# Three vector passes of a weight conversion moved behind a gate's first step, with one POOL sum in place of two halves

## The chip, the cores and the metric

The kernel runs on one core of a Trainium2 chip. The time is the device time of one execution in microseconds (us). The kernel before takes 814.9 us, the median of three executions (814.84 to 814.9).

The core's engines run side by side, each through its own list of instructions in order: TensorE (PE in the profile, its weight loads PEld), VectorE (DVE), ScalarE (ACT), GpSimd (POOL) and SyncE (SP). Semaphores order them against each other. DMAs are issued from the lists of SP, ACT and POOL.

## The reference, cut to what matters

```python
# x (8, 8, 512, 64), state (8, 8, 32, 64); per batch and head:
scores = scale * x @ state.T;  a = softmax(scores);   xread = a @ state
scores2 = scale * state @ x.T; a2 = softmax(scores2); sread = a2 @ x
x = concatenate([xread, sread], axis=2)      # -> (8 * 544, 512) tokens
h = x @ w_in                                 # w_in (512, 2048)
g = h * cos(h)
out = g @ w_out                              # w_out (2048, 512)
```

x and state arrive as float32. w_in and w_out arrive as float64, and the chip computes in float32, so each weight has to be turned from 64 bits into 32 on the way in.

## The kernel before, in words

**Order of the work.** The lists of all engines are written out by hand. A prologue prepares batch 0. Then a loop of 16 steps per batch follows, one step for each slice of 128 of the 2048 hidden features, and 16 more steps for the state tokens. Step s does, in this order of code: PE multiplies the hidden tile (`hidden`, L443) of 128 features by 512 tokens; the gate follows in four parts, ACT's pass that rounds (`gate`, L449), DVE's distance (`gate2`, L452), ACT's magnitude and sine (`gate3`, L457 and L458) and DVE's product (`gate4`, L464). PE's output product of a tile (`output`, L508) comes three or four steps later. Hidden tiles have two PSUM banks, so the hidden product of step s+2 writes the bank that the product (L464) of step s has read.

**Attention** of the next batch is spread over the steps by `plan`: its parts go on the lists at five places of a step, `go(0)` to `go(4)`, where `go(1)` and `go(2)` are ACT's parts and `go(3)` and `go(4)` DVE's. `products` (L295) multiplies a block of w_in by the states, and its copies (L422 on DVE, L424 on ACT) make the weights of the hidden product. `max1`, `max2` (with a small scaling, L327), `spread1`, `shift`, `exps`, `sums` (with L351 and L352), `norm1` and `keep` are the softmax.

**Weight loads.** Eighteen loads (two more at the end) bring w_in and w_out as raw 64-bit words into one of three buffers, on SP (`fetch`, L190). `convert_part` makes 32-bit words of each: ACT takes the high words ("1", L218) and the low words ("2", L221, into `low`), DVE limits ("a", L225), shifts ("b", L227) and puts in the sign ("c", L230), POOL adds the low words ("d", L240). A buffer is fetched anew after "c". Loads 0 to 3 have 512 elements per partition, all later ones 1024. The table `conv_at` gives load 4 + i to a step; steps 0 to 8 and 10 to 14 have one. In its step a load gets "1", "2" and, at the end of the step, "a" and "b"; "c" and "d" come in the next step, between distance and product. From load 4 on POOL's "d" is two instructions of 512.

**Prologue.** All eight heads of batch 0 are loaded on SP; the states of batches 0 to 3 half on ACT, half on POOL; then SP fetches raw loads 0 to 4 and the other states. Raw loads 0 and 1 share a buffer, 2 and 3 another. PE turns three quarters of the tokens, then the states, then the last quarter; scores follow, then matmuls on zeros (`warm`), while DVE and ACT go through softmax and the first conversions.

**Later.** From step 15 on POOL makes sums of blocks of w_out (`blocks`, L775) and differences of gated tiles (L470).

Of the kernel before, what the change touches and what calls it, by code (L numbers as in the profile page):

```python
# [10 lines left out]
I32 = mybir.dt.int32  # L11
U32 = mybir.dt.uint32
ALU = mybir.AluOpType
# [10 lines left out]
def kernel(  # L24
# [8 lines left out]
    nc = tc.nc  # L33
# [5 lines left out]
    NK = Dm // P  # L39
# [43 lines left out]
    x_b = consts.tile([P, NC, H, D], F32)  # L83
# [10 lines left out]
    low = s4.rearrange("p f d -> p (f d)")  # L94
    low = [low[:, 2 * WC * i:2 * WC * i + 2 * WC] for i in range(2)]
    RG = 4 * WC * 2 // S // 2
    raw_at = [g_all[:, NG - RG * (3 - i):NG - RG * (2 - i)] for i in range(3)]
    raw_at = [r.rearrange("p t s -> p (t s)") for r in raw_at]
# [2 lines left out]

    stT = consts.tile([P, B, P], F32)

    def load_x(b):

        src = x[b].rearrange("h (c p) d -> p c h d", p=P)
        for h in range(H):
            nc.sync.dma_start(out=x_b[:, :, h], in_=src[:, :, h])


    zeros = g_all[:, 0]
# [1 line left out]

    load_x(0)
    st_src = state.rearrange("b (k j) n d -> j k n b d", j=2)

    def load_state(half, queues):
        b = slice(4 * half, 4 * half + 4)  # L120
        for k in range(NK):
            for j in range(2):
                queues[j].dma_start(
                    out=st[Ns * k:Ns * k + Ns, b, D * j:D * j + D],
                    in_=st_src[j, k, :, b])
# [7 lines left out]
    acc = [[ops.tile([P, S], F32, name=f"o{m}{ch}") for ch in range(2)]  # L133
           for m in range(2)]

    def states(half, to):
        for i in range(4):
            nc.tensor.transpose(out=to[:, P * i:P * i + P],
                                in_=st[:, 4 * half + i, :], identity=ident)

    def states_kept(half, to):
        dst = slice(4 * half, 4 * half + 4)
        src = to.rearrange("p (b m) -> p b m", b=4)
        nc.vector.tensor_scalar(stT[:, dst], src, 1.0 / TWO_PI, None,
                                op0=ALU.mult)
# [22 lines left out]
    N_LOADS = len(loads)  # L168
# [5 lines left out]
    n_fetched = 0  # L174

    def fetch(n):
        nonlocal n_fetched
        while n_fetched < n:
            dst, src = loads[n_fetched]
            if f64:  # L180
                m, w = dst.shape[1:]

                at_, c0 = (n_fetched - 2) % 3, 0
                if n_fetched < 4:
                    at_, c0 = n_fetched // 2, n_fetched % 2 * 2 * m * w
                if n_fetched >= N_LOADS:
                    at_ = 3 + n_fetched - N_LOADS
                raw = raw_at[at_].bitcast(I32)[:, c0:c0 + 2 * m * w]
                raw = raw.rearrange("p (m f) -> p m f", m=m)
                nc.sync.dma_start(out=raw, in_=src.bitcast(I32))  # L190
                raws[n_fetched] = raw.rearrange("p m (f w) -> p m f w", w=2)
            else:
                nc.sync.dma_start(out=dst, in_=src)
            n_fetched += 1
# [6 lines left out]
    def convert(i, parts):  # L201

        if i < len(loads) and f64:
            for p in parts:
                convert_part(i, p)
        if "c" in parts and i not in (1, 2) and i + 3 < N_LOADS:
            fetch(max(i + 4, 6))

    def convert_part(i, p):
        raw, dst = raws[i], loads[i][0]
        bits = dst.bitcast(I32)
        m, w = dst.shape[1:]
        c0 = m * w if i in (2, 3) else 0
        e = low[i % 2][:, c0:c0 + m * w].rearrange("p (m f) -> p m f", m=m)
        if p == "1":
            nc.scalar.activation(dst, raw.bitcast(F32)[:, :, :, 1],  # L218
                                 func=ACTF.Abs)
        elif p == "2":  # L220
            nc.scalar.activation(e, raw.bitcast(U32)[:, :, :, 0],  # L221
                                 func=ACTF.Copy, scale=2.0 ** -51, bias=2.0)
        elif p == "a":
            engine = nc.gpsimd if i == 1 else nc.vector
            engine.tensor_scalar(dst, dst, 2.0 ** -15, None, op0=ALU.max)  # L225
        elif p == "b":
            nc.vector.tensor_scalar(bits, bits, 3, None,  # L227
                                    op0=ALU.logical_shift_left)
        elif p == "c":
            nc.vector.scalar_tensor_tensor(out=bits, in0=raw[:, :, :, 1],  # L230
                                           scalar=-2 ** 31, in1=bits,
                                           op0=ALU.bitwise_and,
                                           op1=ALU.bitwise_xor)
        else:


            n = 1 if i < 4 else 2
            for j in range(n):
                r = slice(m * j // n, m * j // n + m // n)
                nc.gpsimd.tensor_tensor(bits[:, r], bits[:, r],  # L240
                                        e.bitcast(I32)[:, r], op=ALU.add)

# [3 lines left out]
    class Attention:  # L248
# [27 lines left out]
        def tokens_kept(self, k):  # L276
            nc.scalar.copy(self.xT[:, k], at[k % 2])

        def all_tokens(self, k0, k1):

            xp = [acc[k // 2][k % 2] for k in range(NK)]
            for k in range(k0, k1):
                for c in range(NC):
                    self.turn_x(k, c, xp[k])
                if k % 2 == 0:
                    nc.scalar.copy(self.xT[:, k], xp[k])
                else:
                    nc.vector.tensor_copy(self.xT[:, k], xp[k])
# [139 lines left out]
    def part(b, name, *args):  # L428

        if b not in attn:  # L430
            attn[b] = Attention(b)
        getattr(attn[b], name)(*args)
        if (name, args) == ("reads", (1,)) and b + 1 < B:
            load_x(b + 1)


    class Tile:
# [2 lines left out]
    def hidden(t):  # L440
        t.hp = hps.tile([P, S], F32, name="h")[:, 0:t.n]
        for i in range(t.kn):
            nc.tensor.matmul(out=t.hp, lhsT=t.lhs(i), rhs=t.rhs(i),  # L443
                             start=(i == 0), stop=(i == t.kn - 1))

    def gate(t):

        t.q = msb.tile([P, S], F32, name="q")[:, 0:t.n]
        nc.scalar.activation(t.q, t.hp, func=ACTF.Copy, bias=MAGIC)  # L449
# [11 lines left out]
    def gate4(t):  # L461
        t.slot = g_free.pop(0)
        t.g = g_all[:, t.slot, 0:t.n]
        nc.vector.tensor_tensor(t.g, t.hp, t.q, op=ALU.mult)  # L464
# [7 lines left out]
    MAIN, SIDE = 0, 1  # L472
# [195 lines left out]
    def warm(n, to):  # L668

        for _ in range(n):  # L670
            nc.tensor.matmul(out=to, lhsT=zeros[:, 0:P], rhs=zeros, start=True,
                             stop=True)

    fetch(5)
    load_state(1, (nc.sync, nc.sync))
    warm(2, at[0])
    a0 = attn[0] = Attention(0)
    a0.all_tokens(0, 3)
    states(0, at[0])
    states_kept(0, at[0])  # L680
    a0.all_tokens(3, 4)
    a0.scores()
    warm(7, acc[SIDE][1])
    convert(0, "12ab")
    convert(1, "12a")
    a0.max1()
    a0.spread1()
    a0.shift()
    a0.exp1()
    convert(1, "bcd")  # L690
    a0.sums()
    convert(0, "cd")
    a0.spread1()
    convert(2, "12")
    a0.norm1()
# [3 lines left out]
    convert(2, "abcd")  # L699
    a0.max2()  # L700
    a0.exp2()
    convert(3, "ab")

# [83 lines left out]
    for step, t in enumerate(tiles()):  # L789
        s = step % NF  # L790
        if s == 0 and t.b < B:
            steps = plan(t.b)
        todo = [p[s] if t.b < B else [] for p in steps]

        def go(n):
            for p in todo[n]:
                part(*p)

        last, conv = conv_at.get(step - 1, -1), conv_at.get(step, -1)
        if step == 0:  # L800
            last = 3
        if step == B * NF + (0 if f64 else 8):
            fetch(N_LOADS + 2)
        hidden(t)
        go(0)
        if step == 4:
            states(1, acc[SIDE][1])
        gate(t)
        gate2(t)
        go(1)  # L810
        go(3)
        if last >= 0:
            convert(last, "cd")
        if conv >= 0 and not todo[1]:
            convert(conv, "1")
        gate3(t)
        if later:
            later.pop(0)()
        gate4(t)
        if conv >= 0 and todo[1]:  # L820
            convert(conv, "1")
        if t.pair is not None:
            sums(t)
        if step == 5:
            states_kept(1, acc[SIDE][1])
        go(2)
        if conv >= 0:
            convert(conv, "2")
        go(4)
        if conv >= 0:  # L830
            convert(conv, "ab")
        if step in block_at:
            blocks(*block_at[step])
        if t.pair is not None:
            sums2(t)
        while len(line) >= (LAG if step >= NH else LAG + 1):
            output(line.pop(0))
        line.append(t)
# [32 lines left out]
```

## Time and profile before

| | |
|---|---|
| median of three runs | 814.9 us |
| the profiled execution's own time | 814.84 us |
| its span, first to last instruction | 813.0 us |
| PE busy | 778.6 us (96%) |
| DVE busy | 434.5 us (53%) |
| ACT busy | 398.3 us (49%) |
| POOL busy | 183.4 us (23%) |
| mean granted TensorE clock | 0.987 |

A line of the timeline gives the start, the duration, the engine, the line of the code, the operation, the tile written and the tiles read, the shapes and how many instructions are merged (x2); in brackets stands the idle time of the engine before it and what ended it. The line of slices gives the busy share in tenths in 40 equal parts of the span. The chain that ended last is followed back from the last instruction to what released each step. In the waits, a line names who waited, for whom, and the total, the number and the longest.

### The profile page before, as it was taken

What the parts mean: (1) busy time and instruction counts of PE and PEld (TensorE: products, weight loads), DVE (VectorE), ACT (ScalarE), POOL (GpSimd) and SP (SyncE); (2) the same over time, 40 slices, a digit from 0 to 9 for tenths busy, and PEclk for the clock granted to TensorE, in tenths of its full rate; (3) what the DMA queues carried; (4) which work ended last, traced back from release to release, by engine and by line L of the source; (5) the groups of instructions that cost most, each with busy time, mean ns of one, the idle gap of its engine ahead of it and who ended that gap; (6) DMA issues with size and microseconds to landing.
All of it is one profiled execution on the core that took longest, in us unless ns stands there. A gap on an engine that the chain in (4) does not pass through costs nothing.

```text
span 813.0 us, 7602 instructions
## 1 busy us (share of the span) xinstructions
PE 778.6 (96%) x2738; PEld 349.3 (43%) x2738; DVE 434.5 (53%) x671; ACT 398.3 (49%) x644; POOL 183.4 (23%) x135
## 2 busy tenths in 40 slices
PE   7889779989999999999999999999999999999997
PEld 3333234344444444444444344444344444455553
DVE  5799896662354446753365356743654455432431
ACT  3867766544447354644464445644474445322222
POOL 3343248776000000262000000541000003620200
PEclk9799999999999999999999999999999999999999
DMA  8474350010010211120011110120100113100021
GB/s 233 155 212 152 104 154 15 13 38 14 1 26 3 51 26 27 20 59 1 0 27 30 38 23 14 34 45 1 16 10 0 27 26 69 62 1 13 14 39 38
DMA packets 111653, 37.19 MB, mean 46 GB/s; under 512 B 103616, under 2 KB 103616, under 8 KB 111616
## 3 DMA queue, kind: packets, MB, share of 16 engines
q1 hardware_dynamic: 110912, 36.45, 18.6%
q8 instruction: 21, 0.34, 0.2%
q10 hardware_dynamic: 576, 0.13, 0.1%
q0 software_dynamic: 128, 0.13, 0.1%
q14 instruction: 16, 0.13, 0.1%
HBM read 27.79 MB, written 8.91 MB: 45 GB/s over the span
## 4 chain that ended last, share of the span: by engine, by line
PE 78%; DVE 11%; ACT 8%; issue 1%; DMA 1%; POOL 0%; SPq 0%; DVEq 0%; POOLq 0%; ACTq 0%
PE o L508 42%; PE h L443 25%; PE at L295 4%; PE o L625 3%; DVE q L452 2%; PE at L382 2%; ACT q L458 1%; PE at L268 1%; DVE g_all L464 1%; ACT q L457 1%; DVE xT L315 1%; DVE aT L359 1%; DVE w_in L225 1%; ACT xT L341 1%; ACT aT L336 1%
## 5 line engine op out<-in xcount | busy, mean ns | idle before, releaser
L443 PE MATMUL h<-aT,sw 128*128 128x512 f32 x512 | 248.3, 608 | 15.4 <-DVE g_all L464 12.4
L508 PE MATMUL o<-g_all,w_out 128*128 128x512 f32 x512 | 238.9, 604 | 4.5 <-DVE sw L422 2.9
L470 POOL TENSOR_TENSOR g_all<-g_all 128x512 f32<-128x512 f32 x80 | 112.2, 1424 | 460.5 <-DVE g_all L464 455.5
L449 ACT ACTIVATE q<-h 128x512 f32<-128x512 f32 (+1 forms) x144 | 82.2, 571 | 269.3 <-PE h L443 269.3
L452 DVE SCALAR_TENSOR_TENSOR q<-q,h 128x512 f32<-128x512 f32 (+1 forms) x144 | 94.4, 655 | 208.9 <-ACT q L449 208.9
L508 PE MATMUL o<-g_all,s 128*128 128x512 f32 x384 | 177.3, 598 | 0.0
L464 DVE TENSOR_TENSOR g_all<-h,q 128x512 f32<-128x512 f32 (+1 forms) x144 | 94.9, 659 | 139.2 <-ACT q L458 138.9
L443 PEld LDWEIGHTS h<-aT,sw 128*128 128x128 f32 x512 | 98.4, 195 | 145.2 <-issue 111.6
L508 PEld LDWEIGHTS o<-g_all,w_out 128*128 128x128 f32 x512 | 94.1, 191 | 126.8 <-issue 120.1
L457 ACT ACTIVATE q<-q 128x512 f32<-128x512 f32 (+1 forms) x144 | 87.5, 608 | 104.3 <-DVE q L452 104.2
L508 PEld LDWEIGHTS o<-g_all,s 128*128 128x128 f32 x384 | 70.3, 190 | 88.4 <-issue 83.6
L458 ACT ACTIVATE q<-q,halfpi 128x512 f32<-128x512 f32 (+1 forms) x144 | 100.5, 698 | 4.5
L240 POOL TENSOR_TENSOR w_out<-w_out,s 128x512 int32<-128x512 int32 x20 | 26.7, 1354 | 84.9 <-DVE w_out L230 67.8
L470 DVE TENSOR_TENSOR g_all<-g_all 128x512 f32<-128x512 f32 x48 | 33.2, 692 | 1.6
L443 PE MATMUL h<-sT,w_in 128*128 128x256 f32 x128 | 30.2, 379 | 0.0
L424 ACT COPY sw<-at 128x512 f32<-128x512 f32 x48 | 25.7, 588 | 9.0 <-PE at L295 9.0
L625 PE MATMUL o<-w_out,g_all 128*128 128x512 f32 x64 | 29.6, 592 | 0.0
L240 POOL TENSOR_TENSOR w_in<-w_in,s 128x512 int32<-128x512 int32 x16 | 21.5, 1362 | 33.1 <-DVE w_in L230 30.1
L443 PEld LDWEIGHTS h<-sT,w_in 128*128 128x128 f32 x128 | 24.3, 190 | 10.1 <-issue 6.7
L514 DVE SCALAR_TENSOR_TENSOR held<-o,held 128x512 f32<-128x512 f32 x40 | 25.5, 682 | 3.7 <-PE o L508 3.7
L295 PE MATMUL at<-w_in,stT 64*32 64x512 f32 x384 | 26.1, 601 | 0.0
L535 DVE STREAM_TRANSPOSE ot<-held 128x512 f32<-128x512 f32 x32 | 22.2, 695 | 0.0
(84 smaller groups left out, 469.6 us busy)
## 6 DMA issues: line engine op xcount, KB each, us to landing
out_dram<-ot SPq DMA_DIRECT2D x136, 64.0 KB, 2.0
x_b<-in_x_dram SPq DMA_DIRECT2D x64, 128.0 KB, 2.9
g_all<-in_moe_w_out_dram SPq DMA_DIRECT2D x8, 1024.0 KB, 5.1
g_all<-in_moe_w_in_dram SPq DMA_DIRECT2D x6, 1024.0 KB, 5.2
g_all<-in_moe_w_in_dram SPq DMA_DIRECT2D x4, 512.0 KB, 6.0
x_b<-in_moe_w_out_dram SPq DMA_DIRECT2D x1, 1024.0 KB, 5.9
xT<-in_moe_w_out_dram SPq DMA_DIRECT2D x1, 1024.0 KB, 8.0
s<-in_state_dram SPq DMA_DIRECT2D x8, 32.0 KB, 7.1
```

The costliest lines, as they stand in the source:

```text
L240: nc.gpsimd.tensor_tensor(bits[:, r], bits[:, r], e.bitcast(I32)[:, r], op=ALU.add)
L295: nc.tensor.matmul(out=(to or at)[j][Ns * k:Ns * k + Ns, 0:n], lhsT=w[D * j:D * j + D, self.b, Ns * k:Ns * k + Ns], rhs=r(slice(D * j, D * ...
L424: nc.scalar.copy(dst, to[j][:, 0:c1 - c0])
L443: nc.tensor.matmul(out=t.hp, lhsT=t.lhs(i), rhs=t.rhs(i), start=(i == 0), stop=(i == t.kn - 1))
L449: nc.scalar.activation(t.q, t.hp, func=ACTF.Copy, bias=MAGIC)
L452: nc.vector.scalar_tensor_tensor(out=t.q, in0=t.q, scalar=MAGIC, in1=t.hp, op0=ALU.subtract, op1=ALU.subtract)
L457: nc.scalar.activation(t.q, t.q, func=ACTF.Abs)
L458: nc.scalar.activation(t.q, t.q, func=ACTF.Sin, bias=halfpi, scale=-TWO_PI)
L464: nc.vector.tensor_tensor(t.g, t.hp, t.q, op=ALU.mult)
L470: engine.tensor_tensor(out, a, b, op=ALU.subtract)
L508: nc.tensor.matmul(out=acc[bank][ch], lhsT=w[:, i, P * ch:P * ch + P], rhs=g.g, start=(i == 0), stop=(i == NH - 1))
L625: nc.tensor.matmul(out=acc[MAIN][i], lhsT=t.g[:, P * i:P * i + P], rhs=w_out[:, :, t.f, :], start=(n == 0), stop=(n == NF - 1))
```

## The change

- **Conversions in the loop.** "a" and "b" leave the end of their load's own step. They now stand in the next step directly ahead of "c" and "d", between distance and product, one step after ACT's "1" and "2". Load 3's "a" and "b" move from the prologue's end into step 0.
- **POOL's sum** is one instruction for every load.
- **Prologue.** The heads of batch 0 go by turns on SP and ACT, so ACT's state loads stand behind four heads. All tokens are turned before the states. Three raw loads are fetched at first, each into its own buffer, and load i + 3 is fetched after "c" of load i, for every i. Each load uses the first part of its `low` buffer, so load 2 shares it with load 0, load 3 with load 1. "c" and "d" of load 0 stand ahead of "b", "c" and "d" of load 1. Six warming matmuls stand in place of seven.

```diff
-    def load_x(b):
+    def load_x(b, queues):
         src = x[b].rearrange("h (c p) d -> p c h d", p=P)
         for h in range(H):
-            nc.sync.dma_start(out=x_b[:, :, h], in_=src[:, :, h])
+            queues[h % 2].dma_start(out=x_b[:, :, h], in_=src[:, :, h])
...
-    load_x(0)
+    load_x(0, (nc.sync, nc.scalar))
...
-                at_, c0 = (n_fetched - 2) % 3, 0
-                if n_fetched < 4:
-                    at_, c0 = n_fetched // 2, n_fetched % 2 * 2 * m * w
+                at_ = n_fetched % 3
                 if n_fetched >= N_LOADS:
                     at_ = 3 + n_fetched - N_LOADS
-                raw = raw_at[at_].bitcast(I32)[:, c0:c0 + 2 * m * w]
+                raw = raw_at[at_].bitcast(I32)[:, 0:2 * m * w]
...
-        if "c" in parts and i not in (1, 2) and i + 3 < N_LOADS:
-            fetch(max(i + 4, 6))
+        if "c" in parts and i + 3 < N_LOADS:
+            fetch(i + 4)
...
-        c0 = m * w if i in (2, 3) else 0
-        e = low[i % 2][:, c0:c0 + m * w].rearrange("p (m f) -> p m f", m=m)
+        e = low[i % 2][:, 0:m * w].rearrange("p (m f) -> p m f", m=m)
...
-            n = 1 if i < 4 else 2
-            for j in range(n):
-                r = slice(m * j // n, m * j // n + m // n)
-                nc.gpsimd.tensor_tensor(bits[:, r], bits[:, r],
-                                        e.bitcast(I32)[:, r], op=ALU.add)
+            nc.gpsimd.tensor_tensor(bits, bits, e.bitcast(I32), op=ALU.add)
...
-            load_x(b + 1)
+            load_x(b + 1, (nc.sync, nc.sync))
...
-    fetch(5)
+    fetch(3)
     load_state(1, (nc.sync, nc.sync))
     warm(2, at[0])
     a0 = attn[0] = Attention(0)
-    a0.all_tokens(0, 3)
+    a0.all_tokens()
     states(0, at[0])
     states_kept(0, at[0])
-    a0.all_tokens(3, 4)
     a0.scores()
-    warm(7, acc[SIDE][1])
+    warm(6, acc[SIDE][1])
     convert(0, "12ab")
     convert(1, "12a")
     a0.max1()
     a0.spread1()
     a0.shift()
     a0.exp1()
+    convert(0, "cd")
     convert(1, "bcd")
     a0.sums()
-    convert(0, "cd")
     a0.spread1()
...
     a0.exp2()
-    convert(3, "ab")
...
         if last >= 0:
-            convert(last, "cd")
+            convert(last, "abcd")
         if conv >= 0 and not todo[1]:
             convert(conv, "1")
         gate3(t)
...
         if conv >= 0:
             convert(conv, "2")
         go(4)
-        if conv >= 0:
-            convert(conv, "ab")
```

More of the change, by code (lines that the diff above doesn't have):

```diff
@@ L277, in tokens_kept, with all_tokens @@
             nc.scalar.copy(self.xT[:, k], at[k % 2])
-        def all_tokens(self, k0, k1):
+        def all_tokens(self):
             xp = [acc[k // 2][k % 2] for k in range(NK)]
-            for k in range(k0, k1):
+            for k in range(NK):
                 for c in range(NC):
```

## The prediction

> **What bounds the kernel now.** I read the page's busy line and slices first, then the waits up to 140 us, the chain that ended last, and the timelines of DVE, POOL and PE.
>
> ```profile
> PE 778.6 (96%) x2738; PEld 349.3 (43%) x2738; DVE 434.5 (53%) x671; ACT 398.3 (49%) x644; POOL 183.4 (23%) x135
> ...
> PE   7889779989999999999999999999999999999997
> ...
> DVE  5799896662354446753365356743654455432431
> ```
>
> A slice is 20.3 us. PE is short of work only in the first six (0 to 122 us) and briefly in the ninth; from 125 us it sets the pace. The change lies almost wholly in those 122 us, so its worth is how much earlier or later PE gets its work there. The waits of that stretch say for whom PE waits (us in total, times, longest):
>
> ```profile
> PEld h L443 <- DVE g_all L464: 14.0, 7, 3.5
> ...
> PE h L443 <- DVE g_all L464: 8.2, 5, 2.7
> ...
> PE o L508 <- POOL w_out L240: 1.6, 1, 1.6
> ```
>
> The hidden product of step s+2 (L443) reuses the bank that the gate product of step s (L464) sets free. The chain shows what holds L464:
>
> ```profile
> 100.18 0.60 DVE g_all L464
> 100.78 1.37 DVE w_out L225
> ...
> 102.17 0.04 DVE w_out L227
> 102.21 1.53 issue
> 103.74 0.69 DVE q L452
> ...
> 104.45 0.64 ACT q L457
> ...
> 105.11 0.72 ACT q L458
> ```
>
> Limit and shift of the next load stand behind the product and ahead of the next distance (L452), and take 2.9 us here. Alone they take 0.69 each (55.10 and 62.46). The reason is POOL, seen in these two timelines:
>
> ```profile
> 59.35 2.52 POOL L240 TENSOR_TENSOR w_in<-w_in,s 128x512 int32<-128x512 int32 x2 [2.42 <-DVE w_in L230]
> ```
> ```profile
> 60.73 1.70 DVE L225 TENSOR_SCALAR w_out<-w_out 128x1024 f32<-128x1024 f32 x1
> 62.46 0.69 DVE L227 TENSOR_SCALAR w_out<-w_out 128x1024 int32<-128x1024 int32 x1
> ```
>
> POOL's sum ends at 61.87 and the limit at 62.43, 0.56 later: the limit waited for POOL's running instruction. L464, L452 and the copies of L422 keep their 0.69 and 0.64 beside POOL. Over 14 loads limits and shifts took 17.6 + 15.4 us where 28 x 0.69 = 19.3 would do: 13.7 us of waiting. PE itself is slow after a longer pause:
>
> ```profile
> 49.84 2.89 PE L508 MATMUL o<-g_all,w_out 128*128 128x512 f32 x4 [1.61 <-POOL w_out L240]
> ...
> 112.94 1.98 PE L443 MATMUL h<-aT,sw 128*128 128x512 f32 x4 [1.41 <-DVE g_all L464]
> ...
> 119.36 3.51 PE L443 MATMUL h<-aT,sw 128*128 128x512 f32 x4 [2.72 <-DVE g_all L464]
> ```
>
> After pauses of up to 1.52 us four matmuls take 1.98; after 1.61, 2.72 and 2.90 they take 2.9 to 3.5, at a granted clock of 0.67 and 0.55.
>
> **The change, part by part.** All sums are against the profiled run's own 814.84 us (span 813.0 and 1.84 around it), 0.06 below the median of 814.9.
>
> Plain steps. In one, DVE now runs distance, limit, shift, sign, product. POOL starts 0.15 after a sign (64.89 to 65.03). Its one sum of 1024 elements has no row; bounds are L775, 1024 float elements, 2.36, and two halves, 2 x 1.27 = 2.54; I take 2.45, between them. From one sign's end to the next: 0.15 + 2.45, limit's remainder 0.55, shift 0.72, sign 1.21 = 5.1, with product, ACT's pass and the next distance (0.6 + 0.6) under POOL's sum. Before, signs of plain steps ended 5.37 to 5.67 apart (100.18, 105.55, 111.22). ACT's own round (0.49 + 1.05 + 0.65 + 0.74 + 1.10 = 4.0) is shorter. The limit's wait holds shift, sign and product behind it on DVE, and through the product PE's hidden s+2 and ACT's pass on it. Where attention work of 1.2 us or more stands ahead of the limit, POOL is done and limit and shift cost 0.7 each.
>
> Prologue: 0, bounds -0.5 and +2. SP issues four heads (2.3 us) in place of eight, so load 0, for which ACT waits at 10.07, comes earlier. ACT issues eight DMAs (0.53 each, from x4 in 2.13), so its table load moves from 2.88 to 5.0 and ends at 6.3, where its first copy began at 6.14. Its state loads now queue behind four heads; the states' transposes, at 8.17 before, stay near 8.2 if they land by 8. Signs 0 and 1 with shift 1 (0.69 + 0.42 + 0.69 = 1.80) overrun the exponential (1.06) by 0.74, but sign 0 leaves the way after the sums (0.6). PE's one warming matmul less (6.28 / 7 = 0.9) lies beside DVE's chain. Load 3 is issued at sign 0 (about 16), behind SP's state loads, and at 6.0 us to land it is there at 22; ACT needs it by 23.3 so that exp2 keeps 24.65. That is a cover of 1.3 us, and each us beyond it costs one. Load 4 (sign 1, 17, lands by 23) is read at 26.5, load 5 (sign 2, 23, lands by 29) at 33.8: covered. Load 2's low words now wait for sum 0 (to 17.4), hidden since ACT's next copy waits for sum 1 (18.7).
>
> Steps 0 to 5. Limit and shift 3 (0.41 + 0.43) run under ACT's table load; sum 3 ends 30.2 (29.3 before). Step 1: distance to 32.4, copies 0.75, limit, shift and sign 4 (0.7 + 0.7 + 1.2) to 35.7 (34.6). Sum 4 lasts to 38.3, limit 5 to 38.85, sign 5 to 40.7 (40.0). Sum 5 is whole at 43.3, PE's products 44.5, their copies 44.5 to 45.8 (44.27 to 45.55): DVE, busy there before, idles 2.5 us behind the copy. Keep, then limit, shift, sign 6 bring 50.0, against 48.38, and sum 6 ends at 52.6. The first output matmul waited only for its first half, at 49.84; it now starts at 52.6 after a pause of 4 us, slow. Out and hidden 5 take 5.4 as before (49.84 to 55.24), so to 58.1. ACT's pass had begun at 56.04, so the distance of step 5 comes at 58.75 against 57.40: +1.3.
>
> Steps 5 to 9. ACT sets steps 6 and 7: from its pass at 58.1 two copies (0.55), magnitude and sine (1.4), both load passes (1.1) lead to 63.5 and the distance at 64.0; again so to 69.4 (63.07 and 68.76 before). Step 7: distance to 70.0, copies and maxima 2.5, limit, shift and sign 2.6 to 75.1, product, second maximum to 77.0; its scaling (L327, 0.83 at 74.80, held by POOL until 75.6) is held again, till sum 10 ends at 77.7. Distance 8 is at 77.75 (76.87); spread 1.25, limit to sign 2.6, product 0.65 and subtraction 1.25 give distance 9 at 84.1 (83.65): +0.45 is left. There the order lets all of it pass ACT's table load and exponentials: the distance of step 10 is at 90.4 (89.97).
>
> Steps 10 to 16. Limit and shift 13 (1.3) leave the stretch ahead of distance 11: 96.6 (97.20). They come back behind it: distance to 97.3, norm 1.2, limit to sign 2.6, product 0.7 end at 101.8 (100.78). Then two plain steps of 5.05 and one of 6.7 (ACT's pass 0.3, distance 0.7, L351 locked 0.9 until sum 15 ends, keep 1.5, limit 0.7, shift 0.7, sign 1.2, product 0.7) end product 14 at 118.6 (119.30). PE, busy from hidden 13 (slow, 2.9) at 101.9 over 3.3 of products and reads, two hidden and three outputs to 117.4, pauses 1.2 rather than 2.72, so hidden 16 takes 1.9 rather than 3.5. With product 15 at 123.65, hidden 17 starts at 123.7 (125.75): -2.05. I used whole durations; neighbours on DVE that don't depend overlap by 0.06 to 0.09, some 5 of them after step 9: -0.4. From 125 us PE is the bound and keeps this. POOL's block sums move 2 us up with sum 17. Loads 18 and 19 at the end are read three steps later, beside PE. Sum: 814.84 - 2.05 - 0.4 = 812.4.
>
> In the Trainium skill, "TensorE: Matmul & The Clock Gate", "Why this matters for your kernels", the clock falls only after idle gaps above some 3 us, while the rows above show it down after 1.61 and 2.72. By its figure the 2.3 us before hidden 13 cost no clock, PE pauses 2.8 before hidden 16 and isn't slow there either, so an estimate of the sum by it stays at 812.4, and rival 2 falls away; the rows decide.
>
> The same skill, "SBUF — State Buffer", "SBUF: two separate sides", speaks against the one sum: the pair of ports that DVE and POOL share is locked for a whole instruction. No row here shows a DVE pass against a POOL sum of 1024; by that rule the plain step is 5.1 as taken, without it 4.2.
>
> **The rivals.** (1) The time returns as pauses: near 814.9. For it: PE pauses 4 us at the first output, three stretches keep POOL's lock, and the gain rests on steps 12 to 15 alone. If step 9's +0.45 is +2.5, nothing is left.
> (2) Slower by the clock. Products now come 1.3 to 2.5 later after their distances, so PE's pauses, 1.52, 1.05, 1.46 and 1.41 before hidden 10, 11, 13 and 15, may cross the 1.6 where matmuls slow. Each slow start costs 3.51 - 1.88 = 1.6. With four more on the path, 812.4 + 6.4 = 818.8. It decides from three on: 2.4 + 1.6 is the distance to a measurable loss. Against it: ACT's pass does not wait for PE in most of these steps.
> (3) A late prologue: state heads land late on ACT's queue, or load 3 after 23.3. At the upper bound +2: 814.4; it counts as no change.
> (4) The long sum locks DVE no longer than a half does: the three locked stretches of steps 12 to 14 fall by 0.9 each, 812.4 - 2.7 = 809.7. Against it: the limit at 60.73 ended 0.56 after POOL's instruction.
>
> **How the numbers follow.** A measurement of this kernel tells about 0.2%, 1.6 us, from no change: faster is below 813.3, slower above 816.5. My forecast has 0.42 (own range 810.8 to 813.5: 0.38 of it faster, 0.04 the same), rival 1 0.16 (0.14 the same, 0.02 slower), rival 2 0.25, all slower, rival 3 0.07, the same, rival 4 0.10, faster. So faster 0.38 + 0.10 = 0.48, the same 0.04 + 0.14 + 0.07 = 0.25, slower 0.25 + 0.02 = 0.27. The range runs from 809.3, a little below rival 4, to rival 2's 818.8.
>
> **What would show it.** Right: limit near 0.7 at attention steps and 1.2 in plain ones; signs 5.1 apart at steps 11 to 13; the first output at 52.6; hidden 16 without a slow clock; product 14 near 118.6. Wrong: a wait of ACT for load 3 at 22, the gate of step 0 later than 26.0, pauses above 1.6 us before many hidden products, or a sum longer than 2.54.

## The result, and the profile after

The changed kernel takes 819.81 us (median of six executions, 817.97 to 820.05); the kernel before, timed beside it, 814.87. The ratio is 1.0055, with a 95% interval of 1.0042 to 1.0068: slower by 4.9 us, where the forecast was 2.4 faster. The profiled execution has 819.85 us, a span of 818.1 and a mean granted clock of 0.984.

The page of the changed kernel, busy line and slices (a slice is 20.5 us):

```profile
PE 776.4 (95%) x2736; PEld 349.6 (43%) x2736; DVE 428.9 (52%) x671; ACT 397.9 (49%) x644; POOL 178.3 (22%) x119
...
PE   6659789989999999999999999999999999999997
...
DVE  3777896663364435863464446743554355432531
```

DVE is busy 5.6 us less than before, and PE's tail is as full as it was. The waits for POOL did shrink: limits and shifts of loads 4 to 17 take 14.7 + 9.7 us in place of 17.6 + 15.4. But the first three slices fell on PE, and the first and the third on DVE. The waits of the first 140 us (total, times, longest):

```profile
PEld h L433 <- DVE g_all L454: 13.7, 7, 3.8
...
PE h L433 <- DVE g_all L454: 9.4, 5, 3.0
...
ACT L276 <- DMA x_b<-in_x_dram: 8.1, 1, 8.1
...
PE o L498 <- POOL w_out L231: 4.1, 1, 4.1
...
PE at L138 <- DMA s<-in_state_dram: 3.4, 1, 3.4
```

The waits of hidden products for gate products, which the change was forecast to shorten, are about as long as they were (14.0 and 8.2). The third and the fifth line are new: ACT and PE wait for DMAs in the prologue. The chain of the changed kernel there:

```profile
1.85 5.38 DMA x_b<-in_x_dram
7.24 0.02 issue
7.26 0.32 ACTq L123
7.57 0.04 issue
7.62 4.54 DMA s<-in_state_dram
12.16 0.14 issue
12.29 1.10 PE at L138 x4
```

ACT issues its last state loads only once a head has landed (7.24, 7.26); the last then takes 4.54 to land, and PE turns the states at 12.29. Of the 4.12 us in which ACT issues its four state loads (3.94 to 8.06) one issue takes only 0.32 to 0.44. The kernel before turned the states at 8.17, and its first gate pass on ACT stood at 26.00 (timelines of PE and ACT):

```profile
8.17 0.60 PE L138 MATMUL at<-ident,s 128*128 128x128 f32 x4
...
26.00 0.60 ACT L449 ACTIVATE q<-h 128x512 f32<-128x512 f32 x1
```

In the changed kernel scores follow at 14.26 (9.64 before), the first maximum at 16.29 (11.68). A second loss stands where signs 0 and 1 follow each other; DVE's and POOL's timelines of the changed kernel:

```profile
20.89 1.38 POOL L231 TENSOR_TENSOR w_in<-w_in,s 128x512 int32<-128x512 int32 x1 [7.06 <-DVE w_in L226]
...
21.18 1.64 DVE L226 SCALAR_TENSOR_TENSOR w_in<-g_all,w_in 128x512 int32<-128x512 int32 x1
```

Sign 1 takes 1.64 and ends 0.55 after POOL's sum 0; sign 0, with POOL idle, took 0.68. ACT's first gate pass is 5.5 late, at 31.53:

```profile
31.53 0.59 ACT L439 ACTIVATE q<-h 128x512 f32<-128x512 f32 x1
```

From there on the distance to the kernel before grows to 8.6 at step 5 and falls to 4.6 at step 14. Starts of the gate product (DVE's timeline, L464 before, L454 after), with two kernels from the experiments beside them:

| step | before | changed | loop part alone | loop part, halves kept |
|---|---|---|---|---|
| 0 | 30.22 | 35.76 | 30.35 | 30.48 |
| 5 | 59.52 | 68.13 | 62.38 | 60.48 |
| 9 | 85.78 | 92.90 | 87.12 | 84.68 |
| 11 | 100.07 | 106.21 | 100.41 | 97.85 |
| 14 | 118.61 | 123.17 | 117.36 | 113.71 |

Steps 12 to 14 of the changed kernel show the forecast rhythm, on DVE and on POOL:

```profile
106.21 0.68 DVE L454 TENSOR_TENSOR g_all<-h,q 128x512 f32<-128x512 f32 x1
...
107.41 1.95 DVE L221 TENSOR_SCALAR w_out<-w_out 128x1024 f32<-128x1024 f32 x1
...
112.68 1.73 DVE L221 TENSOR_SCALAR w_out<-w_out 128x1024 f32<-128x1024 f32 x1
...
117.51 1.43 DVE L341 TENSOR_SCALAR i<-i 128x2 f32<-128x2 f32 x1
```
```profile
106.44 2.37 POOL L231 TENSOR_TENSOR w_out<-w_out,s 128x1024 int32<-128x1024 int32 x1 [10.95 <-DVE w_out L226]
```

Products are 5.05 apart (106.21, 111.26, 116.31), and the limit waits for a POOL sum of 2.37. On PE, the starts that came after a pause:

```profile
58.94 3.61 PE L498 MATMUL o<-g_all,w_out 128*128 128x512 f32 x4 [4.07 <-POOL w_out L231]
...
88.60 2.87 PE L433 MATMUL h<-aT,sw 128*128 128x512 f32 x4 [2.95 <-DVE g_all L454]
...
106.95 1.98 PE L433 MATMUL h<-aT,sw 128*128 128x512 f32 x4 [2.07 <-DVE g_all L454]
...
123.91 3.55 PE L433 MATMUL h<-aT,sw 128*128 128x512 f32 x4 [2.93 <-DVE g_all L454]
```

Hidden 16 (123.91) is slow after all; hidden 17 starts at 130.34, against 125.75 before.

### The profile page after: what moved, and what is told of

Its sections match the earlier page's. It is cut to its first block, busy times and chain, and to the rows that moved or that the text cites. A ratio compares the mean times of both kernels' runs of the same rounds, so it can differ in the third digit from the quotient of the medians.

```text
span 818.1 us, 7589 instructions
## 1 busy us (share of the span) xinstructions
PE 776.4 (95%) x2736; PEld 349.6 (43%) x2736; DVE 428.9 (52%) x671; ACT 397.9 (49%) x644; POOL 178.3 (22%) x119
## 4 chain that ended last, share of the span: by engine, by line
PE 79%; DVE 10%; ACT 7%; DMA 1%; POOL 1%; issue 1%; ACTq 0%; DVEq 0%; POOLq 0%
PE o L498 43%; PE h L433 25%; PE at L285 4%; PE o L615 3%; PE at L372 2%; DVE q L442 2%; PE at L258 1%; ACT q L448 1%; DVE xT L305 1%; DVE g_all L454 1%; ACT q L447 1%; DVE aT L349 1%; ACT q L439 1%; ACT xT L331 1%; DVE w_in L226 1%; DMA x_b<-in_x_dram 1%
## 5 line engine op out<-in xcount | busy, mean ns | idle before, releaser
L454 DVE TENSOR_TENSOR g_all<-h,q 128x512 f32<-128x512 f32 (+1 forms) x144 | 94.8, 658 | 135.1 <-ACT q L448 134.9
L231 POOL TENSOR_TENSOR w_out<-w_out,s 128x1024 int32<-128x1024 int32 x10 | 23.9, 2390 | 86.3 <-DVE w_out L226 83.6
L231 POOL TENSOR_TENSOR w_in<-w_in,s 128x1024 int32<-128x1024 int32 (+1 forms) x10 | 19.3, 1931 | 42.0 <-DVE w_in L226 39.3
```

The source lines that it names most:

```text
L231: nc.gpsimd.tensor_tensor(bits, bits, e.bitcast(I32), op=ALU.add)
```

## The experiments

**Which part loses.** In the loop two passes moved, limit and shift; the sign, the third in the title, stood between distance and product already. Theory P: the prologue costs some 5 us and the loop part wins about what was forecast. Its rival: the loop part itself loses, by pauses. One kernel has the changed prologue with the old loop, one the old prologue with the changed loop, one the old prologue and the moved passes with POOL's sum left in halves, one POOL's whole sum alone.

prologue_alone, made from the changed kernel:

```diff
-            nc.gpsimd.tensor_tensor(bits, bits, e.bitcast(I32), op=ALU.add)
+            n = 1 if i < 4 else 2
+            for j in range(n):
+                r = slice(m * j // n, m * j // n + m // n)
+                nc.gpsimd.tensor_tensor(bits[:, r], bits[:, r],
+                                        e.bitcast(I32)[:, r], op=ALU.add)
...
+    convert(3, "ab")
...
-            convert(last, "abcd")
+            convert(last, "cd")
...
         go(4)
+        if conv >= 0:
+            convert(conv, "ab")
```

> Only the prologue of the changed kernel; limit and shift stay at the end of a load's step and POOL's sum stays in halves. Theory P (the loss is the prologue's): its first gate pass began 5.5 us later in the changed kernel (31.53 against 26.00) and the loop gave 0.9 back (hidden 17 only 4.6 later), so this kernel is slower than the changed one: 820.0 to 821.0, with the states' transposes again near 12.3. Theory L (the loop loses too, by PE's slow starts): some of the 5 us goes with the loop's part, and this kernel is at 816 to 818.

Measured: 821.01 us (820.32 to 821.48; before 815.48), ratio 1.0068 [1.0056, 1.0080]. The prologue alone costs 5.5.

loop_alone, made from the kernel before:

```diff
-            n = 1 if i < 4 else 2
-            for j in range(n):
-                r = slice(m * j // n, m * j // n + m // n)
-                nc.gpsimd.tensor_tensor(bits[:, r], bits[:, r],
-                                        e.bitcast(I32)[:, r], op=ALU.add)
+            nc.gpsimd.tensor_tensor(bits, bits, e.bitcast(I32), op=ALU.add)
...
-    convert(3, "ab")
...
-            convert(last, "cd")
+            convert(last, "abcd")
...
-        if conv >= 0:
-            convert(conv, "ab")
```

> Only the loop's part of the change (limit, shift and sign between distance and product, one POOL sum), behind the old prologue. Theory P: 813.5 to 814.5, about 0.9 below before. The forecast's own step for this part was 2.4 below, 812.4. Theory L: 816 or more, with at least three more hidden products started on a reduced clock.

Measured: 813.32 us (810.18 to 814.47), ratio 0.9966 [0.9953, 0.9978]: 2.2 faster, about as large as the whole forecast gain. The twelve executions lie far apart, so the trace shows only one of them, that of 812.52. PE's timeline of this kernel:

```profile
53.12 2.57 PE L504 MATMUL o<-g_all,w_out 128*128 128x512 f32 x4 [3.57 <-POOL w_out L237]
...
82.81 1.98 PE L439 MATMUL h<-aT,sw 128*128 128x512 f32 x4 [2.95 <-DVE g_all L460]
...
101.15 2.81 PE L439 MATMUL h<-aT,sw 128*128 128x512 f32 x4 [2.07 <-DVE g_all L460]
...
118.11 1.98 PE L439 MATMUL h<-aT,sw 128*128 128x512 f32 x4 [1.31 <-DVE g_all L460]
...
123.03 1.98 PE L439 MATMUL h<-aT,sw 128*128 128x512 f32 x4
```

The first output is at 53.12, hidden 16 at 118.11 without a slow start, hidden 17 at 123.03, 2.7 ahead of before. The table above shows that the changed kernel follows this one at an almost constant distance: 5.4 at step 0, 5.8 at steps 5 to 14. The whole sum is then 5.8 and 1.5 more for the slow hidden 16 (in the profiled executions 819.85 - 812.52 = 7.3), less the 2.3 of the loop. This sum holds for the two executions profiled; in the ratios, the loop's part is worth about 1 us behind the changed prologue (1.0055 against 1.0068).

middle_halves, the same with the split sum left as it was:

```diff
-    convert(3, "ab")
...
-            convert(last, "cd")
+            convert(last, "abcd")
...
-        if conv >= 0:
-            convert(conv, "ab")
```

> The loop's part with POOL's sum left in halves, behind the old prologue. If POOL holds DVE for one instruction only, the limit in a plain step gets in after the first half (about 0.1 us of waiting instead of 1.1) and the shift waits for the second half, so the step stays near 5.1 to 5.7, and the first output starts on the first half of sum 6, some 1.2 us earlier: 812.5 to 814.5. If the long hold of the one sum is what takes most of the loop's gain, this is at least 1 us below the loop's part with one sum.

Measured: 810.24 us (808.40 to 811.00), ratio 0.9934 [0.9921, 0.9946]: 5.2 faster. That is below the range expected first, and 3.1 below loop_alone, so the long hold of the one sum does cost. PE's and DVE's timelines of this kernel:

```profile
51.94 1.98 PE L508 MATMUL o<-g_all,w_out 128*128 128x512 f32 x4 [3.07 <-POOL w_out L240]
...
80.23 2.98 PE L443 MATMUL h<-aT,sw 128*128 128x512 f32 x4 [3.09 <-DVE g_all L464]
...
109.14 0.34 DVE L351 TENSOR_SCALAR i<-i 128x2 f32<-128x2 f32 x1
```

The table shows where the halves win against the whole sum: 1.9 by step 5, because the first output needs only the first half (51.94 rather than 53.12) and neither it nor hidden 5 is slow there; and 1.1 more from step 11 to step 14, where this line of `sums` (L351 here, L341 in the changed kernel) takes 0.34 rather than 1.44 behind POOL. The 0.7 between steps 5 and 11 was not traced.

end_one_sum, the kernel before with POOL's sum in one and nothing else:

```diff
-            n = 1 if i < 4 else 2
...
+            nc.gpsimd.tensor_tensor(bits, bits, e.bitcast(I32), op=ALU.add)
```

> Only POOL's sum in one, nothing else moved: limit and shift stand right behind the product, so the limit waits for the whole sum (2.35) and the shift then runs free. From sign to sign 0.15 + 2.35 + 0.55 + 0.7 + 0.6 + 1.2 = 5.55, against 5.37 to 5.67 with halves: 814.5 to 816.5, the first output matmul later by up to 1.3. If the one sum is the costly part of the change it is above 816.5.

Measured: 814.82 us, ratio 0.9994 [0.9985, 1.0002]: nothing. The whole sum by itself is worth nothing, and behind the moved passes it costs some 3 (813.32 - 810.24).

**What in the prologue.** Theory S: the state loads stand behind heads on ACT's list. Rival F: the raw loads' new order.

heads_on_sp, the changed kernel with all heads on SP:

```diff
-    load_x(0, (nc.sync, nc.scalar))
+    load_x(0, (nc.sync, nc.sync))
```

> The changed kernel with one thing undone: all eight heads of batch 0 on SP, so ACT's four state loads stand first on ACT. Theory S (the prologue's loss is the states, which ACT issued late behind four heads): the states' transposes fall back from 12.3 to 8.2 to 8.9 and the first gate pass from 31.5 to about 27, and the kernel takes 814 to 815.5, some 4.6 below the changed one. Rival F (the loss is the fetch order: three raw loads at first, loads 3 and 4 fetched after the signs): the kernel stays within 1.5 us of the changed one, above 818.

Measured: 815.46 us (812.00 to 817.44; before 815.08), ratio 1.0000 [0.9986, 1.0015]. Timelines of PE and ACT:

```profile
9.32 0.60 PE L138 MATMUL at<-ident,s 128*128 128x128 f32 x4
...
27.36 0.59 ACT L439 ACTIVATE q<-h 128x512 f32<-128x512 f32 x1
```

The states are turned at 9.32 and ACT's first gate pass is at 27.36, 4.2 earlier than in the changed kernel. Splitting the heads over two queues is the cause of most of the loss; the fetch order alone, with all heads on SP, is not. Of the 1.4 that is left, 0.4 stands at the first maximum (12.12 against 11.68), and 0.95 is sign 1, which still takes 1.64 here.

states_first, the changed kernel with the first state loads ahead of the heads:

```diff
-    load_x(0, (nc.sync, nc.scalar))
...
     load_state(0, (nc.scalar, nc.gpsimd))
+    load_x(0, (nc.sync, nc.scalar))
```

> The changed kernel with the state loads of batches 0 to 3 issued ahead of the heads, the heads still by turns on SP and ACT. Theory S: the states land by 4, but now ACT's heads wait for earlier loads' semaphores, two to four us, so scores start near 10 to 11 and the kernel takes 814.5 to 817. If it is not the order on ACT but the sharing of the DMA engines by two lists that delays the states, they are late here too: 818 or more.

Measured: 821.41 us (820.76 to 822.69), ratio 1.0080 [1.0067, 1.0093]: worse still. Neither expectation came: the states land early, and yet it takes over 818, since now the heads on ACT are late. The chain of this kernel:

```profile
4.04 7.86 DMA x_b<-in_x_dram
11.90 0.04 issue
11.94 2.98 PE o L259 x12
```

Whatever stands second on ACT's list lands late; so it is not the place of the state loads alone. Two theories were left: ACT's second group waits at issue for earlier loads, or it shares the DMA engines with the raw loads, which SP reaches sooner when it issues four heads rather than eight (first raw load at 5.43 before, 3.57 changed, 3.40 here).

four_loads, the changed kernel with batch 0 in four loads of 256 KB, two on each queue, so that fewer issues wait:

```diff
+        if b == 0:
+            for c in range(NC):
+                queues[c % 2].dma_start(out=x_b[:, c], in_=src[:, c])
+            return
```

> The changed kernel with the heads of batch 0 in four loads of 256 KB (one for each 128 tokens of all heads, by turns on SP and ACT) in place of eight. ACT issues two of them and then the states, only two of which wait for an earlier load's counter. Theory S with the wait at issue as its cause: the states land 2 to 4 us earlier than 12.2, the scores start at 11 to 12.5 instead of 14.3, and the kernel takes 816.5 to 818.5. If the time on the shared engines is the cause, not the issue, the states land at 11.5 or later and the kernel takes 819 or more.

Measured: 819.30 us (818.07 to 820.95; before 814.79), ratio 1.0054 [1.0040, 1.0067]. ACT issues its states earlier, from 2.00 to 6.16, and SP the raw loads from 1.85; and every load takes longer to land. The time is on the side of the shared engines, but narrowly, since the executions lie on both sides of 819. The chain:

```profile
1.24 8.57 DMA x_b<-in_x_dram
9.80 0.04 issue
9.85 3.03 PE o L262 x13
```

raws_late, the changed kernel with the raw loads behind SP's state loads:

```diff
-    fetch(3)
     load_state(1, (nc.sync, nc.sync))
+    fetch(3)
```

> The changed kernel with two lines of the prologue exchanged: SP issues the eight state loads of the other batches ahead of the first three raw weight loads, so these start some 5 us later. ACT's order (four heads, then four state loads) and all else stay. Theory of shared engines: the state loads land late because the raw loads of 0.5 MB, issued from 3.57, take the DMA engines' time. Then ACT's four heads land in about 3.7 us rather than 4.7, its four state loads are all issued by about 6.5 and land in about 3.5 us rather than 5.3, and the states' transposes start at 9.5 to 10.8 rather than 12.29. Theory of the wait at issue: ACT's state loads are late because each waits for an earlier load to land before it is issued, whatever SP loads beside; then the last is issued after 7 and the states' transposes start at 11.7 or later. The time itself is no better in either, 818 to 822, since load 0 then lands some 5 us later, at about 14 to 15, and the first two weight passes on ACT wait for it.

Measured: 818.36 us (816.76 to 819.84; before 815.22), ratio 1.0034 [1.0019, 1.0050]. Timeline:

```profile
4.06 4.75 ACTq L123 DMA_DIRECT2D s<-in_state_dram  x4
...
10.35 1.09 PE L138 MATMUL at<-ident,s 128*128 128x128 f32 x4 [1.18 <-DMA s<-in_state_dram]
...
10.92 1.46 SPq L187 DMA_DIRECT2D g_all<-in_moe_w_in_dram  x3
```

With no raw load under way the states are turned at 10.35, 1.94 earlier, inside the range of the shared engines, though ACT issues them no sooner (to 8.81; the expectation of 6.5 was wrong) and its heads still take 4.5 (3.7 was expected). So both theories hold a part: ACT's four state loads still need 4.75 us to be issued, and once issued they land in 3.6 rather than 5.3. The time hardly gains, since load 0 now lands late: ACT waits 3.50 for it until 14.70, and the first maximum, which DVE does behind load 0's limit and shift, starts at 16.20 (16.29). Median landings, from the DMA view of the first 16 us:

| us from issue to landing | before | changed | heads_on_sp | states_first | four_loads | raws_late |
|---|---|---|---|---|---|---|
| heads on SP | 3.7 | 3.9 | 3.9 | 3.3 | 5.0 | 4.0 |
| heads on ACT | - | 4.7 | - | 7.7 | 6.6 | 4.5 |
| states on ACT | 3.1 | 5.3 | 3.1 | 3.2 | 7.3 | 3.6 |
| states on POOL | 3.5 | 4.7 | 3.4 | 3.7 | 7.0 | 5.0 |
| first raw load issued at | 5.43 | 3.57 | 5.24 | 3.40 | 1.85 | 10.92 |

Set one behind the other, the states are turned at 8.17 before, 9.32 with all tokens first, 10.35 with the states behind heads on ACT as well, 12.29 with the raw loads beside them as well. These steps of 1.2, 1.0 and 1.9 are rough: in raws_late SP's eight small state loads run where the raw loads ran, and how much of the 1.0 is the wait at issue and how much the traffic beside it was not separated.

**The second loss in the prologue.** Theory: sign 1 takes 1.64 because POOL's sum 0 runs beside it; with sign 0 behind the sums, as in the kernel before, about 1 us comes back.

sign0_late, the changed kernel with this order:

```diff
-    convert(0, "cd")
     convert(1, "bcd")
     a0.sums()
+    convert(0, "cd")
```

> The changed kernel with sign and sum of load 0 back behind the softmax sums. In the changed kernel sign 1 took 1.64 in place of 0.69, since POOL's sum 0 ran beside it. Theory S with that term: the first gate pass comes 0.9 earlier, and the kernel takes 818.5 to 819.2, against 819.8. If sign 1's wait is covered by the exponential, it stays at 819.8.

Measured: 818.92 us (817.07 to 819.10; before 815.08), ratio 1.0043 [1.0031, 1.0055]. In this kernel load 3 is fetched over load 0's words before sign 0 reads them, so a part of w_in gets the signs of load 3. sign0_after_sums mends that by fetching loads 3 and 4 only behind sign 0:

```diff
-        if "c" in parts and i + 3 < N_LOADS:
-            fetch(i + 4)
+        if "c" in parts and i != 1 and i + 3 < N_LOADS:
+            fetch(max(i + 4, 5))
```

> The changed kernel with sign and sum of load 0 behind the softmax sums, and loads 3 and 4 both fetched only after sign 0, so that no raw words are overwritten early. Theory S with its second term (sign 1 waits 0.95 for POOL's sum 0): sign 1 takes 0.69, the softmax's last product of the prologue ends 0.4 to 0.9 earlier (26.3 to 26.8 against 27.2), and the kernel takes 818.7 to 819.4. But loads 3 and 4 are now issued at 23, 2 later: if load 3 lands after ACT needs it, exp2 and the first gate pass wait, and the time is 820 or more.

Measured: 817.87 us (817.31 to 818.55; before 814.79), ratio 1.0035 [1.0023, 1.0047]. DVE's timeline:

```profile
20.43 0.69 DVE L226 SCALAR_TENSOR_TENSOR w_in<-g_all,w_in 128x512 int32<-128x512 int32 x1
...
23.01 0.63 DVE L226 SCALAR_TENSOR_TENSOR w_in<-g_all,w_in 128x512 int32<-128x512 int32 x1
```

Sign 1 (20.43) takes 0.69 again, with sign 0 at 23.01 behind the sums, and ACT's first gate pass comes at 30.40, 1.1 earlier, though ACT now waits 0.62 for load 3.

**A version that beats both.** middle_halves still pauses 3.07 ahead of the first output. early_load6 is middle_halves with the limit, shift and sign of load 6 ahead of the attention copies in step 3:

```diff
+        if step == 3:
+            convert(last, "abcd")
         go(3)
-        if last >= 0:
+        if last >= 0 and step != 3:
             convert(last, "abcd")
```

> The loop's part with POOL's sum in halves and the old prologue (810.2), and in step 3 limit, shift and sign of load 6 stand ahead of the copies that wait for PE's products, so DVE works where it idled 4 us. Sum 6 then ends some 3 to 4 us earlier, and with it the first output matmul, which waited 3.07 us for it. If that wait sets the steps behind it: 807.0 to 809.0. If DVE's total work sets them (copies and keep come later by 2.6): 809.5 to 811.

Measured: 807.24 us (806.49 to 807.73; before 815.08), ratio 0.9904 [0.9891, 0.9917]: 7.8 faster than before. PE's timeline:

```profile
50.71 1.88 PE L508 MATMUL o<-g_all,w_out 128*128 128x512 f32 x4
...
118.65 1.91 PE L443 MATMUL h<-aT,sw 128*128 128x512 f32 x4
```

The first output comes without a pause at 50.71 (51.94 in middle_halves), hidden 17 at 118.65 (119.31): of the 1.2 us at the first output about half is left at the end of the stretch. The medians of the two kernels lie 3.0 apart, the two profiled executions (808.40 and 807.73) only 0.7: these traces show no cause for the rest.

## Why the prediction was wrong

- **"Prologue: 0, bounds -0.5 and +2"** is the step that failed: the prologue costs 5.5. The failing sentence is "the states' transposes, at 8.17 before, stay near 8.2 if they land by 8". They land at 12.16. I gave four more DMAs on ACT only their issue time, 0.53 each, which would have ended at 5.0; the trace shows ACT still issuing state loads at 7.62, since the issue waits for a head to land, and a landing of 5.3 rather than 3.1. And that load 0 "comes earlier" was counted as nothing but a help. In the kernel before, eight heads on SP hold the first raw load back to 5.43, and this cover I did not name; in raws_late, with the raw loads from 10.92, the states are turned 1.94 earlier than in the changed kernel. The prediction's own sign of being wrong, the gate of step 0 later than 26.0, came with 31.53. The Trainium skill, "DMA: Bandwidth & Descriptors", section "Issuing engines are not separate DMA queues", says that DMAs of all issuing engines run on the same 16 DMA engines and interleave, so that a second issuing engine saves only issue time; the landings in the table agree, and go further: in states_first 128 KB heads issued from 0.73 land in 3.3 us, and the same issued from 3.16, beside raw loads, in 7.7.
- **"Signs 0 and 1 with shift 1 (0.69 + 0.42 + 0.69 = 1.80)"**: sign 1 took 1.64, so the sum is 2.75. I had let POOL lock only limits and shifts. The Trainium skill, "SBUF — State Buffer", section "SBUF: two separate sides", which the prediction names, also counts a DVE operation with two SBUF inputs beside a GpSimd operation that reads SBUF; the sign pass is one, and 1.64 beside 0.69 without POOL's sum agrees.
- **Rival 3** named the right condition, that state loads "land late on ACT's queue", and a price nearly three times too small; its +2 was a bound that no row supported.
- **Steps 0 to 5**: first output 52.6 and distance 5 +1.3, in loop_alone 53.12 and +1.8 (59.19 against 57.40). POOL's sum, taken at 2.45, took 2.37. Right, half a microsecond short.
- **Steps 5 to 9 and 10 to 16**: distances 6 to 10 forecast at 64.0, 69.4, 77.75, 84.1, 90.4; in loop_alone 64.42, 69.67, 77.77, 83.87, 90.20. Product 14 ends at 118.05 (118.6), hidden 17 starts at 123.03 (123.7), hidden 16 pauses 1.31 (1.2) and is not slow. The term of -2.4 was right: -2.2 in the median, though single executions lie from 1.0 to 5.3 below the kernel before.
- **Rival 1** (all comes back as pauses) falls with loop_alone's interval, below 1. **Rival 4** (the whole sum locks no longer) falls with the limits of 1.95 and 1.73. **Rival 2** ended on the right side for a wrong reason: from the first output on the changed kernel has three slow starts on this path (58.94, 88.60, 123.91), as many as before (49.84, 91.41, 119.36), and 5.5 stood lost at step 0. The one at hidden 16 took back 1.5 of what loop_alone gained.
- **The rule of 1.6 us** for a slow start does not hold. The same pause of 2.95 was followed by 2.87 at a granted clock of 0.66 in the changed kernel and by 1.98 at 1.00 in loop_alone; the same pause of 2.07 by 1.98 at 1.00 and by 2.81 at 0.69. Within middle_halves 1.98 at 1.00 follows a pause of 3.07, and 2.98 at 0.65 one of 3.09, so a threshold near 3 us does not fit either. The other course that the prediction worked out, full clock at hidden 13 and then a pause of 2.8 without loss ahead of hidden 16, came by half: 1.98 after 2.07, then a pause of 2.93 and 3.55 at 0.54.

## What to carry to other kernels

Before a load is given to a second issuing engine, list what the first engine will issue sooner, and what small loads this will share the DMA engines with: a queue full of small urgent loads can be the cover that keeps large, patient ones away. A prologue's DMA landings have no cost in a busy table; where they move, bound them by the slowest landing seen under load, not by the median. And try the parts of a change apart: here the loop part with the sum in halves was worth 5.2 us, and the whole came out 4.9 slower.

## What the runs showed of the hardware

- Whether four matmuls after a pause of 2.07 to 3.09 us run at full clock isn't decided by the length of the pause (1.98 against 2.81 to 2.98, both ways round). What decides it was not found.
- A sign pass with two SBUF inputs is held by a POOL sum as limits and shifts are: 1.64 beside it, 0.69 without, ending 0.55 after it.
- Loads of 128 KB in pieces of under 512 bytes have median landings of 3.3 and 7.7 us within one kernel (states_first): the first ahead of the raw loads on SP, the others behind state loads on ACT and beside raw loads.
